# Six experts of a mixture sorted by their counts on the chip, with loads addressed by the sorted numbers

## The chip, the cores and the metric

The program runs on one core of one Trainium2 chip, in one launch. The metric is the device time of an execution in microseconds (us); the time of a kernel is the median of its runs. The engines are called by the names of the profile: PE (TensorE matmuls), PEld (its weight loads), DVE (VectorE), ACT (ScalarE), POOL (GpSimd) and SP (SyncE, which here only issues DMAs).

## The reference

Three stages in a row: attention with a learned position bias, a dense gated layer, and a mixture of eight experts with top-1 routing and a fixed capacity. The change is in the third stage, on tokens `x` of shape 1152 x 512:

```python
logits = x @ w_gate                       # 512 x 8
expert_idx = np.argmax(logits, axis=1)
gate_w = softmax(logits) at expert_idx
for i in range(N):                        # in token order
    e = expert_idx[i]
    if counts[e] < capacity:              # capacity = 1152 // 8 * 2 = 288
        disp[e, counts[e]] = x[i]; pos[i] = counts[e]; counts[e] += 1; keep[i] = True
h = np.maximum(np.einsum('ecd,edf->ecf', disp, w1), 0.0)    # 512 -> 1024
y = np.einsum('ecf,efd->ecd', h, w2)                        # 1024 -> 512
out[i] = gate_w[i] * y[expert_idx[i], pos[i]] if keep[i] else 0
```

With the inputs of the setup, the tokens that chose experts 0 to 7 number 45, 15, 80, 18, 0, 551, 443 and 0. Nothing in the program is built for these numbers; they are computed on the chip in each execution.

## The kernel before

Attention and the dense layer come first, with PE at work nearly throughout. The last part of the dense layer is interleaved with the routing: for each group of 128 tokens the kernel finds the expert and the position, and an indirect DMA writes the row (512 values, the gate, the token number) to its place in `disp`, a buffer in the chip's memory with 288 rows for each expert. A last matmul (`ps_c`) sums the choices, and one DVE instruction turns them into eight whole numbers, `cnt` (L775).

Then comes the expert stage, written in its order by hand (`manual_schedule`, from L1103). Each engine loads the eight counts into registers (TENSOR_LOAD, L1109 to L1113), so that each takes the same branches. Eight slots follow, one for each expert in the order of their numbers. A slot has four ways, here called arms:

- no token: nothing but the preparation of the next slot;
- `few1`, `few2`, up to 64 tokens (M1): plain matmuls on the unsplit weights, 64 columns of tokens at a time;
- `mid1`, `mid2`, up to 128 tokens (P): the weights and the tokens are split into a high and a low half, and three products are summed;
- `full`, up to 288 tokens: the same with three row blocks, the third of 32 rows unsplit. Its second and third block of token rows (`xr`) come by POOL's queue.

The branches of a slot stand in this order: no token? (label z, L1133); more than P? (label d, L1134); more than M1? (L1135); the few arm; the mid arm; then at L1141 the second test on P (label f) and the full arm. Each arm ends in a scatter of its output rows (L559, POOL). Hints tell PE's sequencer which branch will be taken; they are marked in the arms by `hint`, and L1228 shows them in the listings.

The transposes of a slot's first 128 token rows (`transpose_x`, L880) are done one slot ahead, `xd` loads (L852) being issued before the loop. The weights of an expert are eight tiles of 512 KB, in three sets of buffers (expert number modulo 3): `raw`, `eraw` and, for the first half of the third set, `praw`. Experts 0 and 1 are loaded whole, and the first half of expert 2, while the dense layer runs; the second half of expert 2 follows at L1106. After slot e, `load_next` loads the weights of expert e + 3 into the set that has come free, if that expert has tokens. `presplit`, called inside a slot, splits the first weights of the next expert where it has more than M1 tokens.

Of the kernel before, what the change touches and what calls it, by code (L numbers as in the profile page):

```python
# [10 lines left out]
F32 = mybir.dt.float32  # L11
# [399 lines left out]
def moe_kernel(ctx, tc, shape, qd, kd, vd, wb, geo, wg, wv, wo, g2, e1, e2, ebase, desc, tri, out, cap):  # L411
# [16 lines left out]
    BIG = 1.0e6  # L428
    WARM = 12
    BATCHES = (2, 4, 6, 7)  # L430
    TINY = float(np.array([0x38100000], np.uint32).view(np.float32)[0])

    cst = ctx.enter_context(tc.tile_pool(name="cst", bufs=1))
# [186 lines left out]
    cnt = cst.tile([P, NE], I32, name="cnt")  # L620
    ones = yp.tile([P, P], F32, name="ones")
    nc.gpsimd.memset(ones, 1.0)

    with tc.tile_pool(name="o_ps", bufs=2, space=PSUM, reuse_waits="tile") as ops_, \
# [121 lines left out]
        def out_proj_and_route():  # L746
            ends = BATCHES
            batches = {b - 1: (a, b) for a, b in zip((0,) + ends, ends)}

            def batch(tg, stage):  # L750
                if tg in batches:
                    stage(*batches[tg])

            jobs = {
                3: [lambda tg: tg > 1 and (route_l(tg - 2), route_gate(tg - 2))],
                5: [lambda tg: tg > 0 and route_a(tg - 1)],
                10: [lambda tg: batch(tg - 2, route_pos)],
                11: [lambda tg: tg > 0 and route_b(tg - 1), lambda tg: batch(tg - 2, route_c)],
            }
            with tc.manual_schedule():  # L760
                for tg in range(TG):
                    out_proj(2, tg, jobs)
                route_l(TG - 2)
                route_a(TG - 1, 2)
                route_gate(TG - 2)
                route_b(TG - 1)
                route_pos(TG - 2, TG - 1)
                route_c(TG - 2, TG - 1)
                route_l(TG - 1)
                route_gate(TG - 1)  # L770
                route_pos(TG - 1, TG)
                route_c(TG - 1, TG)
                ps = mps.tile([P, 512], F32, tag="gv", name="ps_c", bufs=6)
                nc.tensor.matmul(ps[:, :NE], ones, cum[:, TG], start=True, stop=True)
                nc.vector.tensor_copy(cnt, ps[:, :NE])  # L775

        for f in range(NFC):
            if f + 1 < NFC:
                load_gv(f + 1)
            if f % 2 == 1:  # L780
                load_wo(f // 2)
            if f == NFC - 1:
                load_e(0)
            if 1 <= f <= 6:
                for job in zero_jobs[3 * f - 3:3 * f]:
                    job()
            gate_val(f)
            if f == NFC - 1:
                xs.close()
                eps_ = {1: ctx.enter_context(tc.tile_pool(name="ep1", bufs=1, reuse_waits="tile"))}  # L790
                load_e(1)
                load_e(2, 0)
            if f % THIRD == THIRD - 1:
                if f == NFC - 1:
                    out_proj_and_route()
                else:
                    for tg in range(TG):
                        out_proj(f // THIRD, tg)
# [57 lines left out]
    def alloc_xr(e):  # L856
        xr[e] = mp.tile([P, 2, W], F32, tag="xr", name="xr", bufs=3)

    def load_xr(e):
        t = xr[e]  # L860
        o = e * CAP + P
        with tc.If(nio[e] > P):
            from_disp(nc.gpsimd.dma_start(t[:, 0, :], disp[o:o + P, :]))
            from_disp(nc.gpsimd.dma_start(t[:cr - P, 1, :], disp[o + P:o + cr, :]))

    xt = {}

    px = {}

    def alloc_x(e):  # L870
        px[e] = (
            eps.tile([P, 512], F32, tag="x", name="ps_x", bufs=1) if e else eps.tile([P, 512], F32, tag="t", name="ps_x0")
        )
        if e < NE:
            xt[e] = mp.tile([P, KC, P], F32, tag="xt", name="xt", bufs=2)

    def transpose_x(e):
        if e < NE:
# [7 lines left out]
    def hint_next(e):  # L886
        if e < NE:
            with tc.If(ns[e] > 0) as c:  # L888
                with tc.If(ns[e] > P):
                    hint(f"d{e}")  # L890
            with c.Else():
                hint(f"z{e}")
# [21 lines left out]
                wsplit(e, 1)  # L914

    hid = {}

    def few1(e):
        hint(f"f{e}")
        w = weights(e)  # L920
        x = xt[e]
        q = 2
        n, fw = P // q, F2 // q
        nk = fw // P
        ph = []
        for s in range(fw // 256):
            ps = eps.tile([P, 512], F32, tag="h", name="ps_sh")
            for kc in range(KC):
                for g in range(q):
                    f = g * fw + s * 256  # L930
                    nc.tensor.matmul(
                        ps[g * n:(g + 1) * n, :256], x[:, kc, :n], w[f // 256][:, kc, :],
                        start=kc == 0, stop=kc == KC - 1, skip_group_check=True,
                    )
            ph.append(ps)
        with tc.block():
            hint(f"f{e}")
        h = obs[e % 2, 1]
        pt = []
        for s in range(fw // 256):  # L940
            c = slice(s * 256, (s + 1) * 256)
            nc.vector.tensor_scalar_max(h[:, c], ph[s][:, :256], 0.0)
            ps = eps.tile([P, 512], F32, tag="t", name="ps_st")
            for k in range(2):
                o = (2 * s + k) * P
                nc.tensor.transpose(ps[:, k * P:(k + 1) * P], h[:, o:o + P], ident)
            pt.append(ps)
        ht_ = hid[e][2]
        for s in range(fw // 256):
            nc.vector.tensor_copy(  # L950
                ht_[:, 2 * s:2 * s + 2].rearrange("p k g t -> p (k g t)"), pt[s][:, :2 * P]
            )

    def few2(e):
# [10 lines left out]
        for i, (k, g) in enumerate(seq):  # L965
            f = g * nk + k
            for d in range(q):
                nc.tensor.matmul(
                    ps[d * n:(d + 1) * n, :dw], ht_[:, k, g, :], w[4 + f // 2][:, f % 2, d * dw:(d + 1) * dw],
                    start=i == 0, stop=i == len(seq) - 1, skip_group_check=True,  # L970
                )
            if i == len(seq) // 2:
                with tc.block():
                    hint(f"f{e}")
        finish(ps, to, dw)

    def mid1(e):
# [125 lines left out]
    with tc.manual_schedule():  # L1103
        load_xd(0)
        load_xd(1)
        load_e(2, 1)  # L1106
        for e in range(2, NE - 2):
            load_xd(e)
        _, ns = nc.values_load_multi_w_load_instructions(cnt[0:1, :])  # L1109
        _, nva = nc.values_load_multi_w_load_instructions(  # L1110
            cnt[0:1, :], engines=[mybir.EngineType.DVE, mybir.EngineType.Activation]
        )
        _, nio = nc.values_load_multi_w_load_instructions(  # L1113
            cnt[0:1, :], engines=[mybir.EngineType.SP, mybir.EngineType.Pool]
        )
        for e in range(3):
            alloc_xr(e)
            load_xr(e)
        alloc_x(0)

        warm = eps.tile([P, 512], F32, tag="h", name="ps_warm")
        for _ in range(WARM):
# [2 lines left out]
        for t in [t for x in hl for t in x] + [t[:, 0] for t in xs_]:  # L1125
            nc.vector.tensor_copy(t[:, :1], ident[:, :1])
        presplit(0)
        for e in range(NE):
            alloc_x(e + 1)
            transpose_x(e + 1)  # L1130
            hid[e] = [mp.tile([P, NF2, P], F32R, tag=t, name=t, bufs=1) for t in ("mhh", "mhl")]
            hid[e].append(mp.tile([P, F2 // 2 // P, 2, M1], F32, tag="sht", name="sht", bufs=1))
# [10 lines left out]
            with some.Else():  # L1143
                presplit(e + 1)
            if e + 3 < NE:
                alloc_xr(e + 3)
            load_next(e)
            if e < 2:
                load_xd(NE - 2 + e)


def layout(inputs):
# [79 lines left out]
```

## Time and profile before

| | us |
|---|---|
| median of the runs | 591.99 (591.12 to 592.31) |
| the profiled execution, its own time | 588.43 |
| its span, from the first to the last instruction | 586.6 |
| mean granted TensorE clock over the span | 0.961 |
| PE busy | 535.1 (91%) |
| the expert stage: from the last `ps_c` matmul to the end of the span | about 435 to 586.6 |

All times below are counted from the start of the profiled span. The slots can be told from the lines of PE's matmuls: L931 and L968 are the few arm, L988 to L1016 the mid arm, L1037 to L1082 the full arm. L880 are the transposes for a slot, which run before the slot's branches. In the trace a few arm runs in slots 0, 1 and 3, the mid arm in slot 2, the full arm in slots 5 and 6; slots 4 and 7 compute nothing.

### The profile page before, as it was taken

What the parts mean: (1) busy time and instruction counts of PE and PEld (TensorE: products, weight loads), DVE (VectorE), ACT (ScalarE), POOL (GpSimd) and SP (SyncE); (2) the same over time, 40 slices, a digit from 0 to 9 for tenths busy, and PEclk for the clock granted to TensorE, in tenths of its full rate; (3) what the DMA queues carried; (4) which work ended last, traced back from release to release, by engine and by line L of the source; (5) the groups of instructions that cost most, each with busy time, mean ns of one, the idle gap of its engine ahead of it and who ended that gap; (6) DMA issues with size and microseconds to landing.
All of it is one profiled execution on the core that took longest, in us unless ns stands there. A gap on an engine that the chain in (4) does not pass through costs nothing. (4 is left out here: it accounts for less than half of the span.)

```text
span 586.6 us, 10919 instructions
## 1 busy us (share of the span) xinstructions
PE 535.1 (91%) x3864; PEld 424.7 (72%) x3864; DVE 393.5 (67%) x1033; ACT 267.0 (46%) x578; POOL 93.3 (16%) x156
## 2 busy tenths in 40 slices
PE   6799999999999999999999999999979488299894
PEld 2366666666778899989999899997766285187673
DVE  7799999997776599999988475344451352244631
ACT  5677787787666345555343043222221150243420
POOL 0133333333333000000000000000231101210402
PEclk9899999999999999999999999999989879589898
DMA  5897436635331999854312121006119626900101
GB/s 189 293 318 236 142 122 198 197 113 183 110 84 57 286 357 341 297 184 160 108 73 94 50 80 65 1 31 258 46 61 340 234 83 254 322 4 1 44 1 44
DMA packets 49811, 88.87 MB, mean 151 GB/s; under 512 B 7986, under 2 KB 27444, under 8 KB 49728
## 3 DMA queue, kind: packets, MB, share of 16 engines
q1 hardware_dynamic: 48032, 84.11, 42.9%
q0 software_dynamic: 1552, 3.70, 1.8%
q8 instruction: 44, 0.72, 0.5%
q14 instruction: 39, 0.32, 0.2%
q10 hardware_dynamic: 144, 0.02, 0.0%
HBM read 66.73 MB, written 22.28 MB: 152 GB/s over the span
## 5 line engine op out<-in xcount | busy, mean ns | idle before, releaser
L488 PE MATMUL ps_gv<-xh,hl 128*128 128x384 f32 x528 | 135.5, 337 | 1.4 <-ACT hl L471 0.8
L488 PEld LDWEIGHTS ps_gv<-xh,hl 128*128 128x128 f32 x528 | 95.3, 188 | 2.8 <-ACT hl L471 1.5
L488 PE MATMUL ps_gv<-xl,hl 128*128 128x384 f32 x264 | 88.7, 336 | 0.0
L225 POOL TENSOR_SCALAR e_sb<-e_sb,rs 128x576 f32<-128x576 f32 x72 | 58.4, 821 | 127.4 <-DVE rs L221 98.4
L735 PE MATMUL ps_o<-hl,hh 128*128 128x512 f32 x216 | 72.4, 403 | 0.0
L107 DVE TENSOR_SCALAR bt<-geo_sb 128x320 f32<-128x320 f32 (+17 forms) x144 | 69.3, 517 | 0.0
L211 ACT ACTIVATE e_sb<-e_sb,mn 128x576 f32<-128x576 f32 x72 | 55.1, 768 | 15.9 <-DVE mn L203 15.9
L203 DVE CUSTOM_DVE_ANT_0 e_sb<-ps_s,bias_sb 128x576 f32<-128x576 f32 x72 | 51.3, 748 | 13.1 <-PE ps_s L186 5.9
L237 PEld LDWEIGHTS ps_t<-ident,e_sb 128*128 128x128 f32 x324 | 34.6, 142 | 30.8 <-POOL e_sb L225 15.3
L237 PE MATMUL ps_t<-ident,e_sb 128*128 128x128 f32 x324 | 52.0, 288 | 1.5 <-DVE et L246 1.1
L186 PE MATMUL ps_s<-kst,qst 64*128 64x288 f32 x320 | 49.3, 426 | 3.4 <-DVE mn L203 3.4
L488 PEld LDWEIGHTS ps_gv<-xl,hl 128*128 128x128 f32 x264 | 49.6, 188 | 0.1
L735 PEld LDWEIGHTS ps_o<-hl,hh 128*128 128x128 f32 x216 | 40.6, 188 | 10.0 <-issue 1.4
L559 POOL DMA_INDIRECT disp<-y,rsi x9 | 9.0, 1000 | 225.0 <-DVE rs L683 209.8
L735 PE MATMUL ps_o<-hl,hlo 128*128 128x512 f32 x105 | 42.1, 401 | 0.0
L266 PE MATMUL ps_x<-et,vn 128*64 128x128 f32 (+1 forms) x640 | 40.5, 269 | 0.0
L186 PEld LDWEIGHTS ps_s<-kst,qst 64*128 64x128 f32 x320 | 28.2, 186 | 15.3 <-issue 5.2
L471 ACT CAST hl<-dg 128x512 fp32r<-128x512 f32 x34 | 20.4, 620 | 39.0 <-PE ps_o L735 21.6
L498 ACT CAST hh<-sg 128x384 fp32r<-128x384 f32 x36 | 18.4, 511 | 38.3 <-DVE sg L497 38.0
L266 PEld LDWEIGHTS ps_x<-et,vn 128*64 128x64 f32 x640 | 31.7, 136 | 4.4
L248 ACT COPY et<-ps_t 128x384 f32<-128x384 f32 x72 | 31.2, 483 | 1.0 <-PE ps_t L237 1.0
L1059 PE MATMUL ps_h<-dxh,hl 128*128 128x288 f32 x128 | 29.5, 324 | 0.8 <-ACT dxh L458 0.8
(204 smaller groups left out, 910.1 us busy)
## 6 DMA issues: line engine op xcount, KB each, us to landing
raw<-e SPq DMA_DIRECT2D x24, 512.0 KB, 7.8
bias_d<-bo SPq DMA_DIRECT2D x36, 295.5 KB, 2.3
eraw<-e SPq DMA_DIRECT2D x16, 512.0 KB, 7.8
raw<-wo SPq DMA_DIRECT2D x12, 512.0 KB, 5.0
raw<-wg SPq DMA_DIRECT2D x11, 512.0 KB, 4.7
raw<-wv SPq DMA_DIRECT2D x11, 512.0 KB, 6.0
disp<-zero SPq DMA_DIRECT2D x9, 520.0 KB, 7.9
bias_sb<-bias_d SPq DMA_DIRECT2D x16, 288.0 KB, 3.6
```

The source lines that it names most:

```text
L107: nc.vector.tensor_scalar(t[:, :m], dist_sb[:, :m], nbp[:, r:r + 1], None, ALU.max)
L186: nc.tensor.matmul(pss[j][:, half, :HS], qst[c * B + bb][d, p], kst[d, bb * NP + p, half * HS:(half + 1) * HS], start=bb == bbs[0], stop=b ...
L203: nc.vector.tensor_tensor_reduce(out=e[:, j, :].rearrange("p (a n) -> p a n", a=2), in0=ps[:, :, :HS], in1=bias_sb[c, p][:, j, :].rearrang ...
L211: nc.scalar.activation(e[:, j, :], e[:, j, :], AF.Exp, bias=mn[:, j:j + 1], scale=-1.0, accum_out=sm[:, j:j + 1])
L225: nc.gpsimd.tensor_scalar(e[:, j, :], e[:, j, :], rs, 1.0, ALU.mult, ALU.mult)
L237: nc.tensor.transpose(ps[:, n * P:(n + 1) * P], e[:, o:o + P], ident)
L248: nc.scalar.copy(dst, ps)
L266: nc.tensor.matmul(ps[j * D:(j + 1) * D, o:o + n], vn[:, p, bb, jc, j * D:(j + 1) * D], et[:, t0:t0 + n], start=False, stop=jc == NF - 1, ...
L471: lambda: nc.scalar.copy(dh, g),
L488: nc.tensor.matmul(ps[:, :TN], w_[:, n, kc, :], x_[:, kc, t * TN:(t + 1) * TN], start=i == 0, stop=i == 3 * KC - 1,)
L735: nc.tensor.matmul(ps, ht_cols(f, a, tg), wot[f][b_], start=i == 0, stop=i == len(ops) - 1)
L1059: nc.tensor.matmul(ps[:, :CAP], part(e, f // 2, a)[:, kc, f % 2 * P:(f % 2 + 1) * P], x_[:, kc], start=i == 0, stop=i == 3 * KC - 1,)
```

## The change

The first two slots stay experts 0 and 1. The other six are sorted by their counts, falling, by nine small DVE instructions in place of the one CAST: each count gets a small addend that breaks ties, 36 comparisons give each expert its rank, and comparisons of ranks with places pick out the counts and the numbers in order. `row` then holds eight counts (two fixed, six sorted) and six expert numbers. SP and POOL load the numbers into registers as well, and the DMAs of weights and token rows for slots 2 to 7 take their address from them. For this reason no weight of slot 2 is loaded before the counts are known.

With the inputs here, slots 2 to 7 hold experts 5, 6 (full arm), 2 (mid), 3 (few), 4 and 7 (no token). From slot 2 on, a slot's "no token?" test encloses everything after it: once a slot has no token, the branch goes to the end of the program. Within a slot the few arm now comes first behind a test on M1 (label d), and a second test on M1 (label x) encloses the mid arm (label m) and the full arm (label f). The hint inside the few arm names x in place of f; the hint of the next slot is set by M1 in place of P. The tiles `xr`, `xt`, `ps_x`, `mhh`, `mhl`, `sht` become fixed tiles.

```diff
@@ load_e
-            nc.sync.dma_start(raws[k, n], (e1 if n < 4 else e2)[e, n % 4])
+            src = e1 if n < 4 else e2
+            if e < FIX:
+                nc.sync.dma_start(raws[k, n], src[e, n % 4])
+            else:
+                nc.sync.dma_start(raws[k, n], src[bass.ds(ids[e - FIX], 1), n % 4].rearrange("o p n -> (o p) n"))
@@ out_proj_and_route
-                nc.vector.tensor_copy(cnt, ps[:, :NE])
+                few = ps[:, FIX:NE]
+                v.tensor_copy(row[:, :FIX], ps[:, :FIX])
+                v.tensor_tensor(place[:, 0], few, tie[:, 0], ALU.add)
+                v.tensor_tensor(
+                    beat, place[:, 0].unsqueeze(1).to_broadcast([P, NO, NO]),
+                    place[:, 0].unsqueeze(2).to_broadcast([P, NO, NO]), ALU.is_gt,
+                )
+                v.tensor_copy(tie[:, 0], few)
+                v.reduce_sum(place[:, 0], beat, axis=mybir.AxisListType.X)
...
@@ dense layer, last step
                 load_e(1)
-                load_e(2, 0)
@@ expert stage
+    def rows(e, o, n):
+        if e < FIX:
+            return disp[e * CAP + o:e * CAP + o + n, :]
+        return disp[bass.ds(ids[e - FIX] * CAP + o, n), :]
+
     def load_xd(e):
...
-        from_disp(nc.sync.dma_start(xd0[e], disp[e * CAP:e * CAP + P, :]))
+        from_disp(nc.sync.dma_start(xd0[e], rows(e, 0, P)))
@@ hint_next
-                with tc.If(ns[e] > P):
+                with tc.If(ns[e] > M1):
                     hint(f"d{e}")
@@ few1, twice, and few2
-        hint(f"f{e}")
+        hint(f"x{e}")
@@ with tc.manual_schedule():
         load_xd(0)
         load_xd(1)
-        load_e(2, 1)
-        for e in range(2, NE - 2):
-            load_xd(e)
-        _, ns = nc.values_load_multi_w_load_instructions(cnt[0:1, :])
+        _, ns = nc.values_load_multi_w_load_instructions(row[0:1, :NE])
...
+        _, v = nc.values_load_multi_w_load_instructions(
+            row[0:1, NE:], engines=io_, min_val=0, max_val=NE - 1,
...
+        )
+        ids.extend(v)
+        load_e(2)
+        for e in range(2, NE - 2):
+            load_xd(e)
...
+        nest = ExitStack()
         for e in range(NE):
-            alloc_x(e + 1)
+            if e >= FIX:
+                nest.enter_context(tc.If(ns[e] > 0, label=f"z{e}"))
             transpose_x(e + 1)
...
-            with tc.If(ns[e] > 0, label=f"z{e}") as some:
-                with tc.If(ns[e] <= P, label=f"d{e}"):
-                    with tc.If(ns[e] <= M1) as c:
-                        few1(e)
-                        few2(e)
-                    with c.Else():
-                        mid1(e)
-                        mid2(e)
-                with tc.If(ns[e] > P, label=f"f{e}"):
-                    full(e)
+            def arms():
+                with tc.If(ns[e] <= M1, label=f"d{e}"):
+                    few1(e)
+                    few2(e)
+                with tc.If(ns[e] > M1, label=f"x{e}"):
+                    with tc.If(ns[e] <= P, label=f"m{e}"):
+                        mid1(e)
+                        mid2(e)
+                    with tc.If(ns[e] > P, label=f"f{e}"):
+                        full(e)
...
+        nest.close()
```

SP, the issuing engine, between the token rows of slots 0 and 1 and the loop. `xd` is a token-row load, `eraw` and `praw` are weight tiles, TENSOR_LOAD puts counts or numbers into registers. Before:

```order
L852 DMA xd_5139<-disp 128x520
L852 DMA xd_5141<-disp 128x520
L591 DMA eraw_5143<-e 128x1024
L591 DMA eraw_5145<-e 128x1024
L911 UNCONDITIONAL_BRANCH
L591 DMA eraw_5147<-e 128x1024
L591 DMA eraw_5149<-e 128x1024
L852 DMA xd_5151<-disp 128x520
L852 DMA xd_5153<-disp 128x520
L852 DMA xd_5155<-disp 128x520
L852 DMA xd_5157<-disp 128x520
L1109 TENSOR_LOAD cnt
```

And now:

```order
L894 DMA xd_5171<-disp 128x520
L894 DMA xd_5173<-disp 128x520
L950 UNCONDITIONAL_BRANCH
L1147 TENSOR_LOAD row
L1152 TENSOR_LOAD row
L1153 TENSOR_LOAD row
L596 ISA
L596 DMA praw_5246<-e 128x1024
L596 ISA
L596 DMA praw_5248<-e 128x1024
L596 ISA
L596 DMA praw_5250<-e 128x1024
```

The four `eraw` tiles and the four `xd` loads stood ahead of the loads of the counts. Now three register loads come first, then eight weight tiles (five more follow the three shown), each with an ISA instruction that works out its address, and only then the four `xd` loads.

DVE at the end of the routing. `y` is the last gate, `ps_c` holds the counts in PSUM. Before:

```order
L719 SCALAR_TENSOR_TENSOR rsi<-rps,reb,rsl 128x1
L723 RECIPROCAL y<-rsm 128x1
L775 CAST cnt<-ps_c 128x8
L1109 TENSOR_LOAD cnt
L1110 TENSOR_LOAD cnt
L1126 CAST hl_5125<-ident 128x1
```

And now:

```order
L736 SCALAR_TENSOR_TENSOR rsi<-rps,reb,rsl 128x1
L740 RECIPROCAL y<-rsm 128x1
L794 CAST row<-ps_c 128x2
L795 TENSOR_TENSOR place<-ps_c,tie 128x6
L796 TENSOR_TENSOR beat<-place 128x36
L800 COPY tie<-ps_c 128x6
L801 TENSOR_REDUCE place<-beat 128x6
L802 TENSOR_TENSOR beat<-place 128x36
L807 TENSOR_TENSOR pick<-beat,tie 128x36 x2
L811 TENSOR_REDUCE row<-pick 128x12
L1147 TENSOR_LOAD row
L1148 TENSOR_LOAD row
```

One CAST ahead of the loads of the counts has become nine instructions, of which most read what the one before wrote.

PE at the start of slot 2, behind slot 1's last branches. `ps_x` are the transposes of token rows for slot 3. Before:

```order
L911 UNCONDITIONAL_BRANCH
L598 UNCONDITIONAL_BRANCH
L880 MATMUL ps_x<-ident,xd_5153 128x128 x4
L1133 COMPARE_AND_BRANCH
L1134 COMPARE_AND_BRANCH
L1135 COMPARE_AND_BRANCH
L1228 BRANCH_PREFETCH_HINT
L931 MATMUL ps_sh<-praw_4626,xt 64x256
```

And now:

```order
L1182 UNCONDITIONAL_BRANCH
L950 UNCONDITIONAL_BRANCH
L603 UNCONDITIONAL_BRANCH
L1199 COMPARE_AND_BRANCH
L919 MATMUL ps_x<-ident,xd_5264 128x128 x4
L1179 COMPARE_AND_BRANCH
L1278 BRANCH_PREFETCH_HINT
L972 MATMUL ps_sh<-praw_5246,xt_5152 64x256
```

The transposes of the next slot's rows, which stood ahead of the slot's branches, stand behind the "no token?" test (L1199), and one test on M1 (L1179) leads into the few arm where three tests did.

## Rows read from the trace of the kernel before

**Rows 1.** PE timeline, expert stage: start, us, operation, idle before and releaser
```profile
458.36 3.67 PE L968 MATMUL ps_sy<-eraw,sht 128*64 128x256 f32 x32
470.54 1.09 PE L880 MATMUL ps_x<-ident,xd 128*128 128x128 f32 x4 [8.51 <-issue]
486.60 0.40 PE L1016 MATMUL ps_my<-hl,mhh 128*128 128x512 f32 x1
493.04 3.67 PE L968 MATMUL ps_sy<-raw,sht 128*64 128x256 f32 x32
501.34 1.08 PE L880 MATMUL ps_x<-ident,xd 128*128 128x128 f32 x4 [4.62 <-PEq L1141]
...
512.26 1.09 PE L1037 MATMUL ps_dt<-ident,xr 128*128 128x128 f32 x4 [2.28 <-PEq L1134]
...
543.70 0.64 PE L1076 MATMUL ps_y<-eraw,h 128*32 128x128 f32 x16
546.88 0.63 PE L1037 MATMUL ps_dt<-ident,xr 128*128 128x128 f32 x4 [1.96 <-DVEq L1134]
...
577.78 0.64 PE L1076 MATMUL ps_y<-raw,h 128*32 128x128 f32 x16
```

**Rows 2.** PE's long branches and those after slot 0: duration min/median/max, first and last start
```profile
L1141 PEldq COMPARE_BRANCH  x2: 194/338/482, 450.0 to 452.3; - x2
...
L1135 PEldq COMPARE_BRANCH  x1: 4187/4187/4187, 459.7 to 459.7; - x1
...
L1141 PEldq COMPARE_BRANCH  x2: 2837/3065/3293, 464.0 to 467.5; - x2
...
L1133 PEldq COMPARE_BRANCH  x2: 82/3632/7182, 501.4 to 508.9; - x2
...
L1134 PEldq COMPARE_BRANCH  x1: 2759/2759/2759, 509.1 to 509.1; - x1
```

**Rows 3.** Stretches: busy us (count) by engine, then granted clock, DMA share, GB/s
```profile
443.50:452.10 8.60, 8.29 (x72) 5.45 (x72) 1.64 (x4) 0.75 (x2) 1.05 (x5) 1.00 1.00 371
462.10:471.20 9.10, 0.67 (x3) 0.70 (x4) 0.48 (x1) 0.00 (x0) 2.46 (x8) 0.72 0.42 135
471.20:476.30 5.10, 5.10 (x25) 5.10 (x25) 2.19 (x2) 3.52 (x4) 0.00 (x0) 0.50 0.00 0
476.30:487.10 10.80, 10.21 (x59) 8.22 (x57) 6.44 (x8) 5.09 (x7) 0.00 (x0) 1.00 0.32 101
496.80:512.20 15.40, 2.17 (x8) 1.43 (x8) 3.45 (x4) 3.68 (x5) 4.52 (x11) 0.61 0.97 352
512.20:517.30 5.10, 4.69 (x20) 4.24 (x21) 0.89 (x2) 0.75 (x2) 1.47 (x8) 0.50 0.06 23
546.80:551.40 4.60, 4.08 (x20) 3.81 (x21) 0.89 (x2) 0.75 (x2) 3.52 (x9) 0.63 0.36 134
```

**Rows 4.** DVE timeline, dependent small instructions of the routing
```profile
433.62 0.23 DVE L684 SCALAR_TENSOR_TENSOR rsc<-ps_r,rs,desc_sb 128x8 f32<-128x8 f32 x1
433.88 0.16 DVE L685 TENSOR_REDUCE rs<-rsc 128x1 f32<-128x8 f32 x1
```

**Rows 5.** The tile of the counts: duration ns min/median/max
```profile
L775 DVE CAST cnt<-ps_c x1: 146/146/146, 435.7 to 435.7; 128x8 int32<-128x8 f32 x1
L1109 SPq TENSOR_LOAD <-cnt x1: 732/732/732, 445.1 to 445.1; - x1
L1113 SPq TENSOR_LOAD <-cnt x1: 541/541/541, 445.8 to 445.8; - x1
```

**Rows 6.** SP timeline, weight loads of slot 2
```profile
439.88 1.85 SPq L591 DMA_DIRECT2D eraw<-e  x4
```

**Rows 7.** Token-row loads, 430 to 470 us, from issue to landing
```profile
DMA to landing us min/median/max: 2.7/7.6/8.1
```

**Rows 8.** POOL timeline, scatter of slot 0 and last scatter
```profile
453.49 1.08 POOL L559 DMA_INDIRECT out_dram<-ob,su  x1 [3.29 <-DVEq L1141]
580.20 0.97 POOL L559 DMA_INDIRECT out_dram<-ob,su  x1 [0.30 <-issue]
```

More of the change, by code (lines that the diff above doesn't have):

```diff
@@ L430, in moe_kernel @@
     BATCHES = (2, 4, 6, 7)
+    FIX = 2
     TINY = float(np.array([0x38100000], np.uint32).view(np.float32)[0])
@@ L619, in moe_kernel @@
     nc.sync.dma_start(tri_sb, tri)
-    cnt = cst.tile([P, NE], I32, name="cnt")
+    NO = NE - FIX
+    row = cst.tile([P, NE + NO], I32, name="row")
+    tie = yp.tile([P, 2, NO], F32, name="tie")
+    place = yp.tile([P, 2, NO], F32, name="place")
+    beat = yp.tile([P, NO, NO], F32, name="beat")
+    pick = yp.tile([P, 2, NO, NO], F32, name="pick")
+    for i in range(NO):
+        nc.gpsimd.memset(place[:, 1, i:i + 1], float(i))
+        nc.gpsimd.memset(tie[:, 0, i:i + 1], (NO - i) / 16.0)
+        nc.gpsimd.memset(tie[:, 1, i:i + 1], float(FIX + i))
+    ids = []
     ones = yp.tile([P, P], F32, name="ones")
@@ L774, in out_proj_and_route @@
                 nc.tensor.matmul(ps[:, :NE], ones, cum[:, TG], start=True, stop=True)
-                nc.vector.tensor_copy(cnt, ps[:, :NE])
+                v = nc.vector
+                few = ps[:, FIX:NE]
[7 more added lines that the diff above has]
+                v.reduce_sum(place[:, 0], beat, axis=mybir.AxisListType.X)
+                v.tensor_tensor(
+                    beat, place[:, 0].unsqueeze(1).to_broadcast([P, NO, NO]),
+                    place[:, 1].unsqueeze(2).to_broadcast([P, NO, NO]), ALU.is_equal,
+                )
+                for a in range(2):
+                    v.tensor_tensor(
+                        pick[:, a], beat, tie[:, a].unsqueeze(1).to_broadcast([P, NO, NO]), ALU.mult
+                    )
+                with nc.allow_low_precision("whole numbers"):
+                    v.reduce_sum(
+                        row[:, FIX:], pick.rearrange("p a s i -> p (a s) i"), axis=mybir.AxisListType.X
+                    )
         for f in range(NFC):
@@ L916, in moe_kernel @@
     hid = {}
+    hid3 = [mp.tile([P, NF2, P], F32R, name=t, bufs=1) for t in ("mhh", "mhl")]
+    hid3.append(mp.tile([P, F2 // 2 // P, 2, M1], F32, name="sht", bufs=1))
     def few1(e):
-        hint(f"f{e}")
+        hint(f"x{e}")
         w = weights(e)
@@ L936, in few1 @@
         with tc.block():
-            hint(f"f{e}")
+            hint(f"x{e}")
         h = obs[e % 2, 1]
@@ L973, in few2 @@
                 with tc.block():
-                    hint(f"f{e}")
+                    hint(f"x{e}")
         finish(ps, to, dw)
@@ L1105, in moe_kernel @@
         load_xd(1)
-        load_e(2, 1)
+        _, ns = nc.values_load_multi_w_load_instructions(row[0:1, :NE])
+        _, nva = nc.values_load_multi_w_load_instructions(
+            row[0:1, :NE], engines=[mybir.EngineType.DVE, mybir.EngineType.Activation]
+        )
+        io_ = [mybir.EngineType.SP, mybir.EngineType.Pool]
+        _, nio = nc.values_load_multi_w_load_instructions(row[0:1, :NE], engines=io_)
+        _, v = nc.values_load_multi_w_load_instructions(
+            row[0:1, NE:], engines=io_, min_val=0, max_val=NE - 1,
+            skip_runtime_bounds_check_because="a sum of one of the experts' numbers",
+        )
+        ids.extend(v)
+        load_e(2)
         for e in range(2, NE - 2):
             load_xd(e)
-        _, ns = nc.values_load_multi_w_load_instructions(cnt[0:1, :])
[L1110 to L1115, printed above, removed]
         for e in range(3):
-            alloc_xr(e)
             load_xr(e)
-        alloc_x(0)
         warm = eps.tile([P, 512], F32, tag="h", name="ps_warm")
@@ L1127, in moe_kernel @@
         presplit(0)
+        nest = ExitStack()
         for e in range(NE):
-            alloc_x(e + 1)
+            if e >= FIX:
+                nest.enter_context(tc.If(ns[e] > 0, label=f"z{e}"))
             transpose_x(e + 1)
-            hid[e] = [mp.tile([P, NF2, P], F32R, tag=t, name=t, bufs=1) for t in ("mhh", "mhl")]
-            hid[e].append(mp.tile([P, F2 // 2 // P, 2, M1], F32, tag="sht", name="sht", bufs=1))
-            with tc.If(ns[e] > 0, label=f"z{e}") as some:
-                with tc.If(ns[e] <= P, label=f"d{e}"):
-                    with tc.If(ns[e] <= M1) as c:
-                        few1(e)
-                        few2(e)
-                    with c.Else():
+            hid[e] = hid3
+            def arms():
[4 more added lines that the diff above has]
+                    with tc.If(ns[e] <= P, label=f"m{e}"):
                         mid1(e)
                         mid2(e)
-                with tc.If(ns[e] > P, label=f"f{e}"):
-                    full(e)
[L1143 to L1146, printed above, removed]
+                    with tc.If(ns[e] > P, label=f"f{e}"):
+                        full(e)
+            if e < FIX:
+                with tc.If(ns[e] > 0, label=f"z{e}") as some:
+                    arms()
+                with some.Else():
+                    presplit(e + 1)
+            else:
+                arms()
             load_next(e)
```

19 lines of the change are left out of this document (8 added, 11 removed).

## The prediction

> **What bounds the kernel now.** I read the expert stage alone, since nothing before the counts changes but four weight loads that go. First the table of stretches [rows 3], to see where PE is idle and at which granted clock; then PE's timeline at the ends and starts of the slots [rows 1]; then, for each idle time, what PE's sequencer did in it [rows 2]. The reader should see that the dense arms are full of PE work (27 us of matmuls in a row in a full arm) and that the time that can move lies between the arms. The slots end and start so:
>
> Slot 1 (few) ends at 458.36 + 3.67 = 462.03; 8.51 us idle; transposes at 470.54 and the mid arm, to 486.60 + 0.40 = 487.00, that is 16.46, of which 0.73 are the transposes; the few arm of slot 3 to 493.04 + 3.67 = 496.71, with what stands before it 9.71; then 15.55 us to the full arm's first transposes at 512.26; 32.08 to 543.70 + 0.64 = 544.34; 2.54 to 546.88; 31.54 to 577.78 + 0.64 = 578.42; and 8.2 to the end of the span at 586.6 [rows 1]. Together 124.6 us.
>
> Two of the gaps come from PE's sequencer. In the 8.51 us after slot 1 it spent 4.19, 3.29 and 2.84 us in three branches, and in the 15.55 us one branch took 7.18 and another 2.76 [rows 2]. The same branches after slot 0 took 0.19 and 0.48 us [rows 2]. So a branch over an arm that is left out costs either a few tenths or some three to seven us, and the long ones come one after another with nothing but a slot without tokens between them. The 15.55 us hold 2.17 us of PE work in all [rows 3].
>
> **Step 1, the sort.** Nine DVE instructions for one. Two dependent ones of this kind start 0.26 us apart [rows 4]; the one CAST took 0.15 [rows 5]. Seven of the nine wait for the one before: 8 more starts at 0.17 to 0.26 us give 1.4 to 2.1, and a bound below would be overlap of the three that are independent (1.0), one above the slower 36- and 72-element forms that no row shows (2.5). All of it is on the path, for every engine waits for the counts. I take +1.4. The POOL memsets stand early, where POOL is idle.
>
> **Step 2, the loads of slot 2 and the token rows.** SP now does three register loads (0.73 + 0.54 + about 0.55 = 1.8 us, the first two as in [rows 5]; the third of six registers I take as the second of eight), then eight weight tiles at 0.46 us an issue [rows 6], then the token rows of slot 2. An ISA instruction stands ahead of each issue, for which no row has a price: from nothing, if it is hidden under the issue, to as much as one more issue (0.46). I take nothing, as an issue's own time leaves room beside it, and keep the other end for the range. [...]
>
> The 4 MB, at the 371 GB/s that DMA reached while it was full [rows 3], take 11.3 us. With a first issue at about 441.9 (439.0 before, plus 1.1 to 1.4 of the sort, plus the register loads) and some 2 us until the first bytes land (2.7 is the least of the token rows [rows 7]), the rows of slot 2 land at about 455.5, or 456.4 behind the second and third row block of slot 2 (325 KB by POOL's queue, 0.9 us). PE wants them before the few arm of slot 1, at about 454.1 (452.66 before, plus 1.4). So +2.0, with bounds of 0 (the weights give way to the rows, or the rate is higher) and +5 (each issue costs double). The weights themselves are wanted only by the splits in slot 1 and the full arm at about 470: hidden.
>
> **Step 3, the order of the slots.** What goes: the 15.55 us between slot 3 and the first full arm, since no slot without tokens lies between slots with tokens any more. What comes in their place are four boundaries.
>
> Few (slot 1) to full (slot 2), before 8.51: the jump over mid and full of slot 1 (3.29 us as the like one in [rows 2], of which about 1.9 pass while PE still works, since the sequencer is ahead of it: the branch of 4.19 began at 459.7, 2.3 before the arm ended), transposes of 0.7, the jump over slot 2's mid arm (2.84). Together 5.0. Bounds: 1.6, if both jumps are short, and 9.5, if the first costs 4.19 after the lead and the second 7.18.
>
> Full to full: 2.54 as before. Full to mid (slot 3 to 4): transposes 0.7 and the wait for DVE that made 1.96 before [rows 1], of which a part falls under the first matmuls: 2.0 (bounds 0.7 and 6), and 0.3 for the jump over slot 3's mid arm, mostly under the 1.96. Mid to few (slot 4 to 5): the 9.71 with the arm, and a jump over the full arm in front of it, 2.8 less a lead of 1.8, is +1.0 (bounds 0 and +4).
>
> [...] The first full arm keeps 32.08: it started at 0.50 for 5.1 us before [rows 3] and follows a gap now as well.
>
> The end: few is last instead of full. The scatter of slot 0 began 1.46 us after its arm ended (453.49 against 452.03) and the last scatter began 6.4 before the end of the span [rows 8]: 7.9 for 8.2. Two more long jumps (out of slot 5, and out of the nest at slot 6) pass while that scatter lands.
>
> **The sum.** After slot 1: 5.0 + 32.08 + 2.54 + 31.54 + 2.3 + 14.5 + 10.71 + 7.9 = 106.6 for 124.6, -18.0. Ahead of it +1.4 and +2.0. Together -14.6. Against the profiled execution's own 588.43 that is 573.8; the median of the runs is 3.56 higher, so 577.4.
>
> **The rivals.** (A) The long jumps stay and cost the most that the trace shows. At 7.18 us each (it fell where DMA was 97% busy at 352 GB/s [rows 3], against 2.8 to 4.2 with less traffic), the two jumps after slot 1 give 5.3 + 0.7 + 7.2 = 13.2 for 5.0 (+8.2), slot 3's mid arm +4.9, mid to few +4.4 more: 577.4 + 17.5 = 594.9, slower. It decides above a mean of about 6.4 us for the four jumps, of which 5.7 us in all lie under other work. For it: each jump into slot 2's full arm is near DMA traffic for slots 3 and 4. Against it: in slots 3 and 4 no such traffic is left, and the trace has five long jumps of which four are under 4.2. [...]
>
> (B) The dynamic loads are slow: an issue with its address costs 1 us in place of 0.46, so that eight of them take 4.3 more and the token rows land at about 460, 4 us later than I take: 581.5. For it: no row shows such a DMA. Against: SP has nothing else to do.
>
> (C) The hints work: both jumps after slot 1 and the one after mid are short (5.0 becomes 1.6, 1.0 becomes 0) and the token rows are in time (2.0 becomes 0.7): -5.7, 571.7.
>
> (D) The order doesn't come out falling, or slots without tokens are entered: then the 15.55 us stay and steps 1 and 2 are lost, 595.
>
> **Chances.** The forecast (573 to 580.5) 0.62, B 0.15, C 0.14, A 0.06, D 0.03. The range of 570 to 586 holds the forecast, C and most of B and leaves out A and D; the forecast's own is 573 to 580.5. About 0.2% (1.2 us) is what a measurement here can tell from no change. Faster 0.89; within 0.2%, between the forecast and A, 0.04; slower 0.07, from A and D.
>
> **What would show it.** In the profile after: full arms directly after slot 1 and one behind the other, then mid, then few, and none of the 15.55; the counts' register loads about 1.4 later; the transposes of slot 2's rows with an idle time of about 2 us that ends on a DMA; one or two branches of about 3 us between slot 1 and the full arm, and that gap near 5; the mid arm near 14.5 with a granted clock above 0.8 in its first 5 us; about 7.9 us from the last matmul to the end. The forecast is wrong if branches of over 5 us stand at several boundaries, if the token rows come after 458, or if a full arm takes over 33 us because its weights or their splits are late.

## The result, and the profile after

The changed kernel took 585.85 us (median; 583.18 to 592.24) against 591.99: a ratio of 0.9878, with an interval of 0.9851 to 0.9905, some 7 us. In a second measurement it was 0.9900 (0.9869 to 0.9931), some 6 us. The forecast was 577.4, some 14.6 us: the sign was right, and the size was twice what came. One of the five executions, the profiled one, was slow (592.24 us) and stays out of the ratio, so the rows below are from a second profile (e0_changed), with a span of 587.6 us.

PE's timeline in it, at the ends and starts of the slots, the answer to [rows 1]. Columns: start, us, operation, idle time before it and what ended it. L1009 ends a few arm, L1078 begins a full arm and L1117 ends one, L1029 and L1057 begin and end the mid arm; L919 are transposes.

```profile
453.19 3.67 PE L1009 MATMUL ps_sy<-raw,sht 128*64 128x256 f32 x32
461.38 1.09 PE L919 MATMUL ps_x<-ident,xd 128*128 128x128 f32 x4 [4.51 <-DMA xd<-disp]
462.40 2.89 PE L972 MATMUL ps_sh<-eraw,xt 128*64 128x256 f32 x14
...
469.10 3.67 PE L1009 MATMUL ps_sy<-eraw,sht 128*64 128x256 f32 x32
475.53 0.63 PE L919 MATMUL ps_x<-ident,xd 128*128 128x128 f32 x4 [2.75 <-PEq L1182]
480.68 1.09 PE L1078 MATMUL ps_dt<-ident,xr 128*128 128x128 f32 x4 [4.53 <-PEq L1183]
...
513.21 0.64 PE L1117 MATMUL ps_y<-eraw,h 128*32 128x128 f32 x16
...
519.51 1.09 PE L1078 MATMUL ps_dt<-ident,xr 128*128 128x128 f32 x4 [5.07 <-PEq L1183]
...
551.47 0.65 PE L1117 MATMUL ps_y<-raw,h 128*32 128x128 f32 x16
...
554.70 1.18 PE L1029 MATMUL ps_mh<-hl,dxh 128*128 128x256 f32 x8 [2.00 <-DVEq L1179]
...
567.80 0.40 PE L1057 MATMUL ps_my<-hl,mhh 128*128 128x512 f32 x1
...
574.22 3.67 PE L1009 MATMUL ps_sy<-eraw,sht 128*64 128x256 f32 x32
```

The same place in the kernel before, the end of slot 0 and the start of slot 1's few arm:

```profile
448.36 3.67 PE L968 MATMUL ps_sy<-raw,sht 128*64 128x256 f32 x32
...
453.27 3.99 PE L931 MATMUL ps_sh<-eraw,xt 128*64 128x256 f32 x32
```

The order is as intended: few, few, full, full, mid, few, and the 15.55 us between slot 3 and the first full arm [rows 1] are gone. But the boundaries that took their place have idle times of their own. Slot 0's few arm ends at 456.86 and slot 1's begins at 462.40; slot 1's ends at 472.77 and the full arm begins at 480.68; that one ends at 513.85 and the next begins at 519.51. PE's sequencer was in these branches then (duration in ns: min/median/max, then the start of the first and the last), the answer to [rows 2]. In this order: the jump out of slot 0, out of slot 1, over the mid arm of slot 2, over that of slot 3, out of slot 5, and from slot 6 to the end.

```profile
L1182 PEldq COMPARE_BRANCH  x2: 194/2561/4928, 454.8 to 460.1; - x2
...
L1182 PEldq COMPARE_BRANCH  x3: 68/191/4042, 470.7 to 476.3; - x3
...
L1183 PEldq COMPARE_BRANCH  x1: 3770/3770/3770, 476.5 to 476.5; - x1
...
L1183 PEldq COMPARE_BRANCH  x1: 4188/4188/4188, 514.8 to 514.8; - x1
...
L1182 PEldq COMPARE_BRANCH  x1: 3151/3151/3151, 576.0 to 576.0; - x1
...
L1199 PEldq COMPARE_BRANCH  x2: 201/2452/4703, 579.3 to 584.3; - x2
```

All six are long. The forecast had the one in front of the second full arm mostly under other work, and the last two under the last scatter. Stretches of the same profile, the answer to [rows 3] (busy us and count by engine, then the granted clock, the DMA share, GB/s):

```profile
472.80:480.70 7.90, 0.65 (x5) 0.47 (x5) 0.48 (x1) 0.59 (x1) 2.89 (x10) 0.83 1.02 397
480.70:486.00 5.30, 4.95 (x21) 4.46 (x22) 0.89 (x2) 0.75 (x2) 0.00 (x0) 0.50 1.03 404
...
519.50:525.00 5.50, 5.14 (x22) 4.66 (x23) 0.89 (x2) 0.86 (x3) 1.32 (x7) 0.50 0.06 18
554.70:568.20 13.50, 13.03 (x80) 11.03 (x80) 8.56 (x8) 7.96 (x10) 3.49 (x7) 1.00 0.13 47
```

Both full arms now start at a granted clock of 0.50 (over their first 5.3 and 5.5 us), with idle times of 4.5 and 5.1 us ahead of them in PE's timeline; the mid arm, behind 2.0 us, ran at 1.00 throughout.

The sum of the forecast against this profile, in us:

| term | forecast | this profile |
|---|---|---|
| sort: start of the last `ps_c` matmul to the warm-up matmuls | +1.4 | +1.4 (3.35 for 1.97) |
| slot 0 to slot 1 | +2.0 | +4.3 (5.54 for 1.24) |
| few arm of slot 1 | 0 | +1.6 (10.37 for 8.76) |
| slot 1 to the first full arm | 5.0 | 7.9 |
| first full arm | 32.1 | 33.2 |
| between the full arms | 2.5 | 5.7 |
| second full arm | 31.5 | 32.6 |
| full to mid, with the jump over slot 3's mid arm | 2.3 | 2.6 |
| mid arm | 14.5 | 13.5 |
| mid to few, and the few arm | 10.7 | 9.7 |
| end of PE's work to the end of the span | 7.9 | 9.7 |

The right column makes the stage 2.3 us shorter than before, where the timed runs show 6 to 7. Each profile is of one execution: this one was the slowest of its six runs (589.29 us, the median 586.78), and that of the kernel before lay 3.6 us below its median. Executions differ ahead of the stage, too. Here is the first stretch of 40 us (clock, DMA share and GB/s at the end of the row) of the kernel before as first profiled:

```profile
0.00:40.00 40.00, 29.86 (x223) 14.36 (x223) 32.45 (x104) 24.77 (x52) 6.32 (x14) 0.96 0.77 266
```

and of the same kernel profiled again (e7_before_again), with the same clock of 0.87 as in the changed kernel's second profile:

```profile
0.00:40.00 40.00, 30.06 (x192) 13.29 (x193) 29.90 (x92) 21.74 (x44) 5.36 (x12) 0.87 0.76 257
```

The last `ps_c` matmul starts at 434.89 in the first of these, at 438.50 in the second and at 438.24 in the changed kernel: where the stage begins in a single profile is uncertain by 3.6 us. The timed runs decide on sizes, the profiles on places.

### The profile page after: what moved, and what is told of

The parts are those of the page before. It is cut to its first block, busy times and chain, and to the rows that moved or that the text cites. A ratio compares the mean times of both kernels' runs of the same rounds, so it can differ in the third digit from the quotient of the medians.

```text
span 590.6 us, 11062 instructions
## 1 busy us (share of the span) xinstructions
PE 539.5 (91%) x3860; PEld 425.7 (72%) x3860; DVE 395.0 (67%) x1041; ACT 266.5 (45%) x577; POOL 97.9 (17%) x174
## 5 line engine op out<-in xcount | busy, mean ns | idle before, releaser
L186 PE MATMUL ps_s<-kst,qst 64*128 64x288 f32 x320 | 51.5, 440 | 3.8 <-DVE mn L203 3.8
```

Of the source, the lines that this page charges most:

```text
L186: nc.tensor.matmul(pss[j][:, half, :HS], qst[c * B + bb][d, p], kst[d, bb * NP + p, half * HS:(half + 1) * HS], start=bb == bbs[0], stop=b ...
```

## The experiments

Ratios are to the kernel before, from runs on the same chip. For the changed kernel that is 0.9900 (0.9869 to 0.9931, 586.78 us), and 0.9878 in the first measurement.

**e0_changed** and **e7_before_again**: both kernels once more, unedited.

> The changed kernel as it is, for a second profile. Theory 1 (what was hoped for is lost inside the expert stage: token rows of slot 2 behind 4 MB of weights, jumps over an arm of about 4 us each, a late jump to the end): the last ps_c matmul ends near 435 us as before the change, the time is near 584, and the stage after it lasts some 147 us. Rival 2 (the dense stage itself became longer, by POOL's memsets or other transfers there): ps_c ends near 439 as in the profile at hand, and the stage lasts some 151.

> The kernel before, for a second profile. Both theories: the first 150 matmuls end anywhere from 32.5 to 36 us, as they did over the profiles of the changed kernel; the stage after the last ps_c matmul lasts 150 to 153 us again.

`ps_c` at 438.2 in the changed kernel looks like rival 2; 438.5 in the kernel before, without the change, speaks against it. The stage took 149.4 us in the one and 153.3 in the other (151.7 in the first profile of before), one execution each.

**e1_rows_first**

```diff
-        load_e(2)
         for e in range(2, NE - 2):
             load_xd(e)
+        load_e(2)
```

> The four token-row loads of slots 2 to 5 stand ahead of the eight weight tiles of slot 2. Theory 1: the rows land some 10 us earlier, the idle time of 5.1 us in front of slot 1's few arm falls to the 2 to 2.5 us that the jump out of slot 0 (4.0 us, begun 2 us before the arm ends) then exposes, and the arm no longer runs at half clock: 3 to 5 us faster than the changed kernel. Rival 2: the jump alone holds PE for as long and the clock falls anyway: within 1 us.

Ratio 0.9916 (0.9891 to 0.9941): no gain. The transposes in front of slot 1's few arm (PE timeline) and PE's jump out of slot 0 in this kernel:

```profile
455.43 0.82 PE L919 MATMUL ps_x<-ident,xd 128*128 128x128 f32 x4 [2.52 <-DMA eraw<-e]
...
L1182 PEldq COMPARE_BRANCH  x2: 194/2090/3985, 450.9 to 455.1; - x2
```

The gap is 3.3 us in place of 5.5, and the jump, begun at 450.9 and 4.0 us long, ends at 454.9, 0.6 before the transposes, so that it now holds PE. The row names a weight load as the last releaser; the like row of e11, with 2.60 us of idle time, names PE's sequencer. The few arm behind it took 11.3 us, not less. Rival 2 of this run stands: one wait lay over the other.

**e2_no_mid_2_3**

```diff
-                    with tc.If(ns[e] <= P, label=f"m{e}"):
-                        mid1(e)
-                        mid2(e)
-                    with tc.If(ns[e] > P, label=f"f{e}"):
+                    if e not in (2, 3):
...
+                    else:
                         full(e)
```

> Slots 2 and 3 have no mid arm (65 to 128 tokens aren't computed for there; no such slot occurs with these inputs). Theory 1: the jumps over it, 4.0 us after slot 1 and 4.3 between the full arms, go, of which 4.0 and 3.2 stood on the path: 6 to 8 us faster than the changed kernel, the gap few to full 8.0 becomes 4, full to full 5.8 becomes 2.6. Rival 3: other jumps become long in their place as the code moves, and the gain is under 3 us.

Ratio 0.9724 (0.9699 to 0.9750), 575.63 us: some 11 us faster than the changed kernel, more than theory 1 has. PE's timeline, end of slot 1 and the starts of the full arms:

```profile
467.34 3.67 PE L1009 MATMUL ps_sy<-eraw,sht 128*64 128x256 f32 x32
...
473.60 0.63 PE L919 MATMUL ps_x<-ident,xd 128*128 128x128 f32 x4 [2.58 <-PEq L1182]
474.65 1.08 PE L1078 MATMUL ps_dt<-ident,xr 128*128 128x128 f32 x4 [0.42 <-PEq L1179]
...
509.82 0.63 PE L1078 MATMUL ps_dt<-ident,xr 128*128 128x128 f32 x4 [1.96 <-DVEq L1179]
```

From slot 1 to the full arm it is 3.6 us in place of 7.9, and the second full arm follows the first (507.27) after 2.6 in place of 5.7: together 7.4. Another 2.9 came at the end (6.8 for 9.7); that was not foreseen. One PE jump of 3.6 us is left there of two, but what sets the end is POOL (see the part on why below): it stands still for 0.4 us behind its branch out of the slots, where it was 3.3.

**e3_six_slots**

```diff
-        for e in range(NE):
+        for e in range(NE - 2):
             if e >= FIX:
```

> The loop has six slots, so slots 6 and 7 (no tokens with these inputs) aren't in the program. Theory 1: the jump from slot 6's test to the end (4.7 us) goes, the end waits for the last scatter alone: from the last matmul to the end of the span about 7.9 in place of 10.1, 2 us faster than the changed kernel. Rival 3: the jump out of slot 5 lasts longer in its place, no difference.

Ratio 0.9892 (0.9864 to 0.9919): not told apart from the changed kernel. In its profile the end is shorter than theory 1 has it (5.9 us from the last matmul to the end of the span, for 9.7), but a gain of that size does not show in the timed runs.

**e4_all_three**: the three edits together.

> Rows first, no mid arm in slots 2 and 3, and six slots, all at once (leaves out 65 to 128 tokens in slots 2 and 3, and slots 6 and 7). Theory 1, narrowed by what the single ones gave (rows first alone nothing, no mid arm 10 us, six slots 1 us): about 574, and the gap after slot 0 is then set by the jump out of it (2.5 us in place of 5.7). Rival 3 (another jump takes each one's place): no faster than the kernel without the mid arms by more than 0.5 us.

Ratio 0.9692 (0.9661 to 0.9724), 572.64 us, near the 574 of theory 1: 3 us below e2 by the medians, with intervals that overlap, so rival 3 is not ruled out. The end took 5.5 us, the way from slot 0 to slot 1 3.6.

**e5_full_before_mid**

```diff
-                    with tc.If(ns[e] <= P, label=f"m{e}"):
-                        mid1(e)
-                        mid2(e)
                     with tc.If(ns[e] > P, label=f"f{e}"):
                         full(e)
+                    with tc.If(ns[e] <= P, label=f"m{e}"):
+                        mid1(e)
+                        mid2(e)
... (the three hints inside the mid arm go, too)
```

> In each slot the full arm stands ahead of the mid arm, and the hints inside the mid arm go. Theory 1: the full arms of slots 2 and 3 begin without a jump over the mid arm (4.0 us after slot 1 and 3.1 between the full arms go); the mid arm of slot 4 begins behind a jump over a full arm, of which 2 are hidden under DVE's 2.0: 4 to 6 us faster than the changed kernel. Rival 3: the jump over the mid arm behind a full arm is as long as the one before it was: no gain.

Ratio 0.9856 (0.9834 to 0.9879), 583.82 us: 3 us faster than the changed kernel by the medians, with intervals that overlap. PE's timeline, the starts of the two full arms and of the mid arm:

```profile
476.77 1.09 PE L1069 MATMUL ps_dt<-ident,xr 128*128 128x128 f32 x4 [0.55 <-PEq L1170]
...
512.13 0.63 PE L1069 MATMUL ps_dt<-ident,xr 128*128 128x128 f32 x4 [1.78 <-DVEq L1170]
...
550.60 2.05 PE L1029 MATMUL ps_mh<-hl,dxh 128*128 128x256 f32 x8 [4.22 <-PEq L1174]
```

The jumps moved as expected: 4.0 us (for 7.9) and 3.1 (for 5.7) lie in front of the full arms, and an idle time of 4.2 in front of the mid arm, where 2.0 stood. Some of the gain is paid back there, so the size was missed. Rival 3 falls: behind a full arm the jump over the mid arm took 0.2 us.

**e6_order_given**, **e9_slot2_known** and **e11_sort_static** peel off the sort and the dynamic addresses.

```diff
# e6: loads by a written order, no sort
+    ORDER = (0, 1, 5, 6, 2, 3, 4, 7)
+            nc.sync.dma_start(raws[k, n], src[ORDER[e], n % 4])
+        ns, nva, nio = ([v[i] for i in ORDER] for v in (ns, nva, nio))
# e9: slot 2's weights alone by a known number
-            if e < FIX:
-                nc.sync.dma_start(raws[k, n], src[e, n % 4])
+            if e < FIX or e == 2:
+                nc.sync.dma_start(raws[k, n], src[5 if e == 2 else e, n % 4])
# e11: as e6, with the nine instructions of the sort and its counts
... (all three load the first half of slot 2's weights early again; e6 and e11 the token rows, too)
```

> The order of the experts is written in the program for these inputs; the sort and the numbers' registers go, the first half of slot 2's weights is loaded early and the token rows stand ahead of the counts' registers, all as before the change; slots and arms as in the changed kernel (leaves out the sorting). Theory 1: the sort's 1.4 us go; the rows are in time; the jump out of slot 0 takes some 3 us or less with less traffic, so that the gap after slot 0 is 1.2 to 3 in place of 5.5 and slot 1 runs at full clock: 5 to 8 us faster than the changed kernel, and the jumps over mid stay at 3 to 4. Rival 4 (the sort and the dynamic addresses are what costs, nothing else): 1.4 to 2 us faster.

> The sort, the registers and every other dynamic address stay; only slot 2's weights are loaded by a number written in the program (expert 5), the first half early and the second ahead of the counts, as before the change (leaves out that slot 2's expert is found on the chip). Theory 1 (the 4 MB behind the counts make the rows late and the fetch of the jump's target late): the jump out of slot 0 is below 1 us, as in the kernel with the order given, the gap after slot 0 is 0.6 to 1.3 in place of 4.5 to 5.7, 3 to 5 us faster than the changed kernel. Rival 5 (the sort's late start moves the jump into other traffic all the same): the jump stays near 4 and the gain is below 2.

> The kernel with the order given, but with the sort left in: the counts come sorted from the nine DVE instructions, while every load still takes its address from the order written in the program (leaves out the expert numbers' use). Theory 1 (the sort costs its own 1.4 us and nothing else): 1 to 2 us slower than with the order given, and the jump out of slot 0 stays under 1 us. Rival 5 (what comes later by the sort meets the long fetch): the jump is 3.5 to 5 us again, the gap after slot 0 some 2.3, 3 to 4 us slower than with the order given; then the dynamic addresses have no part in it.

Ratios 0.9886 (0.9861 to 0.9910), 0.9894 (0.9867 to 0.9921) and 0.9894 (0.9871 to 0.9918): none is told apart from the changed kernel. What the sort, the numbers' registers, the dynamic addresses and the 4 MB behind the counts cost, one by one or together, is less than these runs tell apart, some 3 us by the intervals; the 5 to 8 us of e6's theory 1 did not come, though the gap after slot 0 is 1.1 us in its profile in place of 5.5. The jump out of slot 0 in the three, in this order:

```profile
L1145 PEldq COMPARE_BRANCH  x2: 194/444/693, 451.5 to 453.7; - x2
```

```profile
L1183 PEldq COMPARE_BRANCH  x2: 194/1978/3761, 452.4 to 456.4; - x2
```

```profile
L1173 PEldq COMPARE_BRANCH  x2: 194/2128/4062, 455.4 to 459.7; - x2
```

It is short in e6 alone, as it was before [rows 2]. Theory 1 put its length down to the traffic of slot 2's weights; it falls with e9, where those are loaded as before. Why the jump is short in e6 and not in e11, which differ by the sort on DVE, is open. The DMA records go one step further. Between slot 0's first hint and this branch, e6 (444.48:451.45) has an instruction transfer of 16 KB on queue q8, as both profiles of before have; e0, e1, e9 and e11 have none there. In e0 one lies within the jump (454.85:459.78), 2.3 us after it begins. The two rows, e6 and e0:

```profile
q8 instruction: 1, 0.02, 1.0%
```

```profile
q8 instruction: 1, 0.02, 1.5%
```

So where the jump was long, the transfer came behind the branch; what sets its time is not shown. The fetch that the expectations of e9, e10 and e11 speak of was my supposition: no run shows that a jump waits for such a transfer.

**e10_no_hints**

```diff
     def hint(label, taken="LikelyTaken"):
-        tc.mark_branch_hint_location(label, hint=taken, engines=[mybir.EngineType.PE])
+        pass
```

> The changed kernel without any of PE's branch hints. Theory 1 (no hint bears on the jumps that were long): the jumps out of slots 0 and 1, over the mid arm and to the end are as long as they are; only the short jump over a full arm behind slot 4's mid arm becomes 3 to 4 us, so 1 to 3 us slower. Rival 6 (hints already shorten the long ones, or mislead the fetch): 5 us or more slower, or 2 or more faster.

Ratio 1.0081 (1.0053 to 1.0109), 595.43 us: 9 to 11 us slower than the changed kernel, the first half of rival 6. The branches out of slots 0 and 1, and behind slot 4's mid arm:

```profile
L1182 PEldq COMPARE_BRANCH  x2: 190/3488/6786, 451.5 to 458.5; - x2
...
L1182 PEldq COMPARE_BRANCH  x2: 191/3156/6121, 468.2 to 474.6; - x2
...
L1186 PEldq COMPARE_BRANCH  x2: 185/1954/3723, 568.2 to 572.2; - x2
```

The first two took 6.8 and 6.1 us in place of 4.9 and 4.0, the third 3.7 where it was a few tenths. The branch past slot 2's few arm became long as well, 3.5 us for 0.2. So the hints bear on the long jumps, too, without making them short. Here a transfer lies 2.2 us ahead of the jump out of slot 0, which took 6.8 us all the same.

**e8_no_mid_general**: e1 and e2, and the loads of slots 2 and 3 widened so that the full arm can serve 65 to 128 tokens.

```diff
-        with tc.If(nio[e] > P):
+        with tc.If(nio[e] > (M1 if e in (2, 3) else P)):
```

> Rows first, and slots 2 and 3 have the full arm for every count above 64 (the loads of their second and third row block go by the same bound), all eight slots: nothing is left out of the computation. Theory 1: as the kernel without the mid arms, 574 to 575, and some 2 us of the jump to the end stay. Rival 3: more than 578, because the program is laid out otherwise.

Ratio 0.9735 (0.9690 to 0.9780), 575.30 us: it beats both kernels, the one before by 16 us and the changed one by some 10. By its code it leaves nothing out; but no slot 2 or 3 has 65 to 128 tokens with these inputs, so the full arm was not run with such a count. The starts of its full arms:

```profile
471.89 0.63 PE L1078 MATMUL ps_dt<-ident,xr 128*128 128x128 f32 x4 [0.42 <-PEq L1179]
...
505.84 0.63 PE L1078 MATMUL ps_dt<-ident,xr 128*128 128x128 f32 x4 [1.95 <-DVEq L1179]
```

## Why the forecast was right in sign and twice too large

Step 3 failed, at two boundaries. "Few (slot 1) to full (slot 2)" was put at 5.0 us and took 7.9; "Full to full: 2.54 as before" took 5.7. In them lie the jumps over the mid arms of slots 2 and 3, 3.8 and 4.2 us long.

I had the first jump at 2.84. The rest of that boundary's 2.9 us is the jump out of slot 1 (4.0 us for 3.29) and about 1.4 us of short steps between branch, transposes and arm, which the forecast had at nothing. The second jump I had in the wrong place: "0.3 for the jump over slot 3's mid arm, mostly under the 1.96" stands in the forecast under "Full to mid", but slot 3's mid arm is jumped on the way into slot 3's full arm, between the full arms. There the sequencer came to the branch at 514.8, behind the transposes, when the arm in front had ended (513.85). The wait of 1.96 for DVE, which e2 and e8 still show at this place, hid only about 1.1 us of it, and 3.1 were added.

e2 shows that the jumps cost this much: without them the kernel is some 11 us faster than the changed one, and in its profile 7.4 of it stand at these two boundaries and 2.9 at the end. The forecast had 2.84 and 0.3 for the jumps.

One reading behind these prices was incomplete. "Five long jumps of which four are under 4.2" leaves out a sixth in the trace of before, the jump out of slot 3 over its other arms, with which the 15.55 us begin:

```profile
L1141 PEldq COMPARE_BRANCH  x2: 194/3092/5991, 494.8 to 501.0; - x2
```

The other terms. Step 1, the sort, was right: 1.4 us, by these rows of DVE's timeline (the first of the nine instructions and the last). That is its price in the stage; by e11 and e6 the whole time does not move by more than the runs can tell.

```profile
439.03 0.14 DVE L794 CAST row<-ps_c 128x2 int32<-128x2 f32 x1
...
440.30 0.23 DVE L811 TENSOR_REDUCE row<-pick 128x12 int32<-128x72 f32 x1
```

Step 2 was too small, +4.3 us for +2.0. The wait for the rows of slot 2 ended at 461.4, which is 23.1 us after the start of the last `ps_c` matmul; the forecast's 455.5 is 20.6 after it. SP's issues, eight weight tiles and then the rows:

```profile
445.62 2.01 SPq L596 DMA_DIRECT2D praw<-e  x4
447.84 2.26 SPq L596 DMA_DIRECT2D eraw<-e  x4
450.29 4.08 SPq L894 DMA_DIRECT2D xd<-disp  x4
```

From the first tile to the first row it is 0.58 us a tile, where 0.46 was taken, so the ISA instruction ahead of each issue was not free. But e1 and e9, with gaps of 3.3 and 3.1 us after slot 0, show no gain that can be told apart from bringing the rows early, since the jump of 4 us out of slot 0 stands behind. That jump I had not priced at all, from the 0.19 and 0.48 us of [rows 2]. The few arm of slot 1, which the forecast left as it was, took 1.6 us more: the granted clock was 0.82 over its first 5.5 us, where it was 1.00 before, and PE paused for 0.4 us in it. The third register load, on SP, was longer than taken:

```profile
L1153 SPq TENSOR_LOAD <-row x1: 734/734/734, 444.6 to 444.6; - x1
```

0.73 us for six numbers, where about 0.55 was taken, and as the first load takes for eight counts [rows 5].

What was removed was right: the 15.55 us went. Mid to few was short (9.7 us for 10.7), since the jump over slot 4's full arm took 0.35 us and not 2.8. The mid arm took 13.5 for 14.5, and 15.7 before (without the transposes). The 1.2 us that the forecast took off were an estimate, which no run shows by itself; what the profile shows is a clock of 1.00 over the whole arm, where the first 5.1 us had 0.50 before [rows 3]. The arm is 13.2 in e2's profile and 14.8 in e1's, so that it differs by execution. The full arms took 1.1 us more each, by the clock: it was 0.50 for 7.5 us of the first one (480.70:488.20), where that was 5.1 before, and 0.50 in place of 0.63 at the start of the second [rows 3]. So the sign "a full arm takes over 33 us" came (33.2), but not because of weights or splits: PE was idle for 0.35 us within that arm, as before.

The end is later, not earlier (9.7 us for 7.9), but not by PE's jumps. The jump from slot 6 to the end lasted until 584.0, and POOL's long drain, 2.8 us before the end of the span, began at 584.8. What stands ahead of the drain is POOL's own queue, which ran nothing from its branch out of the slots at 580.3 to its next instruction at 583.7:

```profile
L1199 POOLq EVENT_SEMAPHORE  x4: 17/30/43, 583.7 to 583.9; - x4
L1199 POOLq COMPARE_BRANCH  x2: 38/44/50, 580.3 to 584.7; - x2
...
L1278 POOLq DRAIN  x3: 46/103/1955, 584.8 to 587.4; - x3
```

In e3, without slots 6 and 7, the drain begins at 580.2. So the forecast was right that PE's two jumps are covered, and it had POOL's way out of the slots at nothing; what POOL stood for is not shown.

The rivals. A had the long jumps and the wrong price: not 7.18 us but 3.2 to 4.9 for each of them. In each of the six a 16 KB instruction transfer (queue q8) starts, 0.4 to 2.3 us after the branch. Two short ones (0.35 us behind slot 4's mid arm, and 0.69 out of slot 0 in e6) show that a jump over an arm need not be long. B is refuted: an issue took 0.58 us and not 1, and e11, with its addresses written in the program, is not told apart from the changed kernel. C was half true: hints help (e10), but the jumps after slot 1 were not short. The jumps over the mid arms have no hint: the kernel's hints name the labels d, z, x and f, and no run tried one for m. D fell: the order is as intended.

The time of 585.85 us still lies in the wide range of 570 to 586, which was to hold the forecast, C and most of B. As neither B nor C came, that is luck.

## What to carry to other kernels

A branch over code that isn't run can have a price on the engine that jumps, here 3.2 to 4.9 us for six of them. In e0 the one of 4.0 us out of slot 1 began 2.1 us before the arm's matmuls ended, and the one of 4.2 between the full arms 1.0 us after the first full arm: look where the branch starts, not only how long it takes. An arm that is rarely used is better placed where no frequent path has to jump over it, or merged into one that can do its work: merging gained some 10 us here (e8), moving it at most a few (e5). Where two waits lay one over the other, after slot 0, taking away either showed little (e1 0.9916 and e9 0.9894, for 0.9900).

## What the runs showed of the hardware

- The clock granted over the first 40 us was 0.96 in one execution of the kernel before and 0.87 in another, where what followed came 3.6 us later.
- With branch hints (e0) two jumps that stayed long took 4.9 and 4.0 us, without them (e10) 6.8 and 6.1; two others took 0.35 and 0.2 us with, 3.7 and 3.5 without.
- Weight and row loads with an address from a register cost no more time over static ones than these runs can tell (0.9900 for the changed kernel and 0.9894 for e11); an issue took 0.58 us with its address instruction (e0), 0.46 before.
- PE's long jumps came with an instruction transfer behind the branch (six of six in e0); the short jumps out of slot 0, in e6 and the kernel before, had one ahead of it.
